# Moving the division of the masked softmax from GpSimd to VectorE in one batch of a fused attention and expert kernel

## The chip, the cores and the metric

The kernel runs on one core of a Trainium2 chip. A core has five engines that work through their own queues of instructions in order: TensorE (PE in the profile, with its weight loads listed apart as PEld), VectorE (DVE), ScalarE (ACT), GpSimd (POOL) and SyncE (SP, which here issues DMAs only). They meet through semaphores. The metric is the device time of one execution in microseconds (us); lower is better.

## The reference

Three layers follow one another. The first is attention with a threshold: a score counts only if it is within `tau` of the row's maximum. Its shape is 2 batches, 8 heads, 576 positions, 64 elements per head.

```python
scores = scale * np.matmul(q, k.transpose(0, 1, 3, 2))
thresh = np.max(scores, axis=-1, keepdims=True) - tau
scores = np.where(scores >= thresh, scores, -1000000000.0)
scores = scores - np.max(scores, axis=-1, keepdims=True)
attn = np.exp(scores)
attn = attn / (np.sum(attn, axis=-1, keepdims=True) + 1e-09)
return np.matmul(attn, v).astype(np.float32)
```

The second layer takes the 1152 tokens of 512 elements through three matrices to 768, keeps the largest of the three results, and multiplies by `w_out` back to 512. The third mixes four experts (512 to 1024, ReLU, back to 512) by normalised probabilities. All of it is float32.

## The kernel before, in words

**Products.** A float32 matrix product is made of three passes over values that are cut into a high and a low part (`split_term`): high by low, low by high, high by high. ACT makes the high part by a copy that rounds, and POOL or DVE makes the low part by a subtraction. For the weights that is `block`: `hi` on ACT (line 780), `lo` on POOL (line 784). For the experts' hidden values it is line 1202 on ACT and line 1205 on DVE; the experts' outputs are added up on DVE (line 1225).

**Stages.** The tokens are worked in two groups. `attention_fast` does batch 0's attention alone. Then comes a stage in which the products of group 0 (the largest-of-three layer, then the experts) run on TensorE, and `attention_slow` weaves batch 1's attention into them. The end is the rest of group 0 and all of group 1. In the middle stage and in the last one the order on TensorE, VectorE, ScalarE and GpSimd is the program's order (`manual_schedule`); only the SyncE queue's order is chosen by the planner.

**Batch 1's attention.** It has four jobs (pairs of heads) of nine tiles each, 36 steps, and one step more to finish. A tile is 128 query rows by 576 keys. A tile goes through `qk` (scores in PSUM, PE, line 416), `peak` (negated row maximum, DVE, 427), `power` (exponential, ACT, 434), `limit` (threshold, DVE, 430), `weigh` (mask by the threshold, with the row's sum as a second result, DVE, 439), `norm` (reciprocal of the sum on DVE, 445, and the multiplication of the tile by it, 446), `turn` (transposes on PE, 456 and 460), `cut_hi` (high parts of the turned tile on ACT, 502 and 504), `cut_lo` (low parts on DVE, 523 and 525) and, when a group of tiles is complete, `gather` (the product with the values, PE, 549, evacuated by 552 on ACT and 554 on DVE).

Each step of `attention_slow` has four quarters, and a `yield` behind each of them hands over to the product stream, which issues 2100 columns of matmuls and, between them, whatever ACT, DVE and POOL instructions of the products and weights are due. In step i tile i goes through `qk` and `peak` (first quarter), `power` and `limit` (second), `weigh` (third) and `norm` (fourth); tile i-1 goes through `turn` (second), `cut_hi` (third) and `cut_lo` (fourth). `advance` issues the next piece of a job's preparation (`prep`, with DVE lines 243, 256, 257, 283) and of what follows a group (`gather`, `values`).

The argument `swift` of `norm` chooses the engine of the multiplication. In batch 1 it is true for the first two tiles only, so these two run on VectorE and 34 on GpSimd. In batch 0 the call is another one, and the change does not touch it.

PSUM has one buffer for the scores of a tile, one for its transposes, two for smaller pieces and the values' products, and three for the product stream.

Of the kernel before, what the change touches and what calls it, by code (L numbers as in the profile page):

```python
# [22 lines left out]
def fused_kernel(ctx: ExitStack, tc: tile.TileContext, q, k, v, tau, w1, w2, w3, w_out, probs, m_w1, m_w2, out):  # L23
# [118 lines left out]
    def whole_tile(key):  # L142
        if key not in whole:
            whole[key] = mo["whole"].tile([P, N1], F32, tag="whole", name="whole", bufs=KC)
        return whole[key]
# [22 lines left out]
    def load_job(job, names="qkv"):  # L168
        b, p = job.b, job.p
        for nm, src in (("q", q), ("k", k), ("v", v)):  # L170
            if nm not in names:
                continue
            heads = src[b, 2 * p:2 * p + 2]
            load = nc.scalar.dma_start if nm == "v" and b else nc.sync.dma_start
            main = heads[:, 0:MAIN, :].rearrange("h (p c) d -> p h c d", c=NC)
            if nm == "v":
                t = atile([P, 2, NC, D], F32, "vnat")
                load(out=t, in_=main)
            else:
                t = atile([P, NC, 2, D], F32, f"{nm}nat")  # L180
                for h in range(2):
                    nc.sync.dma_start(out=t[:, :, h, :], in_=main[:, h])
            if nm == "q":
                r = diagonal
                for h in range(2):
                    last = nc.sync.dma_start(out=r[h * REM:(h + 1) * REM, h * D:(h + 1) * D], in_=heads[h, MAIN:S, :])
            elif nm == "k":
                r = atile([REM, 2, D], F32, "knrem")
                last = nc.sync.dma_start(out=r, in_=heads[:, MAIN:S, :].rearrange("h r d -> r h d"))
            else:  # L190
                r = atile([P, 1 + (b in TWOFOLD), D], F32, "vnrem")
                if b in TWOFOLD:
                    for h in range(2):
                        last = load(out=r[h * REM:(h + 1) * REM], in_=heads[:, MAIN:S, :].rearrange("h r d -> r h d"))
                else:
                    last = load(out=r[:, 0, :], in_=heads[:, MAIN:S, :])
            job.raw[nm] = (t, r)
        return last
# [142 lines left out]
    def values(job, follower=None):  # L341
        V = atile([P, 2, NC, 2 * D], F32R, "V")
        twofold = job.b in TWOFOLD
        if job.b == 0 or job.p == 0 or twofold:
            at["VR"] = atile([P, 2, 2 * D], F32R, "VR")
            if not twofold:
                nc.gpsimd.memset(f32(at["VR"]), 0.0)
        VR = at["VR"]
        job.v = (V, VR)
        vt, vr = job.raw["v"]  # L350
        vn = vt
        nc.scalar.activation(out=V[:, :, :, 0:D], in_=vn, func=AF.Copy)
        yield
        nc.gpsimd.tensor_tensor(out=V[:, :, :, D:2 * D], in0=vn, in1=f32(V[:, :, :, 0:D]), op=ALU.subtract)
        parts = [(slice(0, P), slice(0, 2))] if twofold else [(slice(h * REM, (h + 1) * REM), slice(h, h + 1)) for h in range(2)]
        for r, h in parts:
            nc.scalar.activation(out=VR[r, h, 0:D], in_=vr[r], func=AF.Copy)
        yield
        for r, h in parts:
            nc.gpsimd.tensor_tensor(out=VR[r, h, D:2 * D], in0=vr[r], in1=f32(VR[r, h, 0:D]), op=ALU.subtract)  # L360
        if follower:
            for _ in range(3):
                yield
            load_job(follower, "v")
# [32 lines left out]
    def qk(st):  # L397
        K12, QS = st.grp.job.kq
        nat = st.grp.job.nat
        st.s = ptile_at("S", [P, 2, 512])  # L400
        for kh in range(2):
            terms = []
            if st.h is None and nat:
                KN, QD = nat
                terms = [(QD[:, y, :], KN[:, x, kh * HS:(kh + 1) * HS]) for y in range(2) for x in range(2)]
            elif st.h is None:
                for h in range(2):
                    lhsT = QS[:, (MAIN, W)[h]:(MAIN, W)[h] + 2 * REM]
                    ko = h * (W + REM) + kh * HS
                    terms += [(lhsT, K12[:, x, ko:ko + HS]) for x in range(2)]  # L410
            else:
                qo = (st.c * P, W + 2 * REM + st.c * P)[st.h]
                ko = st.h * W + kh * HS
                terms = [(QS[:, qo:qo + P], K12[:, x, ko:ko + HS]) for x in range(2)]
            for i, (l, r) in enumerate(terms):
                st.whole = nc.tensor.matmul(st.s[:, kh, 0:HS], lhsT=l, rhs=r, start=i == 0, stop=i == len(terms) - 1)  # L416

    def views(st):
        em = st.em[:, st.col:st.col + S]
        return st.s[:, :, 0:HS], em, em.rearrange("p (a b) -> p a b", a=2)  # L420
# [15 lines left out]
    def weigh(st):  # L436

        sv, _, ev = views(st)
        nc.vector.scalar_tensor_tensor(  # L439
            out=ev, in0=sv, scalar=st.stat["thr"], in1=ev, op0=ALU.is_ge, op1=ALU.mult, accum_out=st.stat["sum"])  # L440

    def norm(st, swift=False):
        em = views(st)[1]
        su, re = st.stat["sum"], st.stat["r"]
        nc.vector.reciprocal(out=re, in_=su)  # L445
        last = (nc.vector if swift else nc.gpsimd).tensor_scalar(out=em, in0=em, scalar1=re, scalar2=one, op0=ALU.mult, op1=ALU.mult)  # L446
        if st.h is None and st.grp.job.b not in TWOFOLD:
            nc.gpsimd.tensor_scalar(
                out=st.em[:, S:S + REM], in0=st.em[:, MAIN:S], scalar1=1.0, scalar2=1.0, op0=ALU.mult, op1=ALU.mult)
        return last  # L450
# [138 lines left out]
    def lined_up(jobs):  # L589
        steps = []  # L590
        for j, job in enumerate(jobs):
            new = job_steps(job)
            for r, st in enumerate(new):
                st.job, st.j, st.r = job, j, r
            steps += new
        return steps
# [87 lines left out]
    def attention_slow(jobs, modes):  # L684

        steps = lined_up(jobs)
        n = len(steps)
        front, back = Queue(), Queue()
        for nm in "kqv":
            load_job(jobs[0], nm)  # L690
        yield SETTLE
        front.add(prep(jobs[0]))
        while not jobs[0].ready:
            front.advance()
            back.advance()
            yield PREPARE
        for p in range(NPAIR):
            nc.gpsimd.tensor_scalar(
                out=whole_tile(("x", p))[:, 0:REM], in0=shared[:, p, :], scalar1=1.0, scalar2=1.0, op0=ALU.mult, op1=ALU.mult)
        yield STACKED  # L700
        for i in range(n + 1):
            st = steps[i] if i < n else None
            old = steps[i - 1] if i else None

            def advance():
                front.advance()
                back.advance()

            if i == 1:

                back.add(values(*jobs[0:2]))
            if st:
                while st.job.ready < 1 + (st.h == 1):
                    front.advance()
                if st.j + 1 < len(jobs):
                    if st.r == LOAD_B:
                        load_job(jobs[st.j + 1], "qk")
                    if st.r == PREP_B:
                        front.add(prep(jobs[st.j + 1]))
                qk(st)  # L720
                peak(st)
            advance()
            yield
            if st:
                power(st)
                limit(st)
            if old:
                turn(old)
            advance()
            yield  # L730
            if old:
                cut_hi(old, next(modes) if old.h is not None else "dve")
            if st:
                weigh(st)
            advance()
            yield
            if st:
                norm(st, i < 2)
            if old:
                cut_lo(old)  # L740
                if old.last:
                    back.add(gather(old.grp))
                    if old.r == 2 * NC and old.j + 1 < len(jobs):
                        back.add(values(*jobs[old.j + 1:old.j + 3]))
            advance()
            yield
        while back.q:
            back.advance()
            yield
# [659 lines left out]
```

## Time and profile before

| | |
|---|---|
| median of three runs | 705.01 us (704.23 to 705.45) |
| profiled execution | 705.1 us |
| its span, first to last instruction | 703.3 us |
| PE busy | 688.2 us, 98% |
| DVE busy | 475.5 us, 68% |
| ACT busy | 365.3 us, 52% |
| POOL busy | 487.1 us, 69% |

The profile is one execution as the hardware profiler recorded it. Its page gives each engine's busy time; matmuls are pipelined and their ends are modelled, so the start-to-start distance of two matmuls says more of PE's pace than its busy share. A group of instructions is written as line, engine, operation, output and inputs by the program's names of tiles, shape, and count. A timeline row is the start in us from the span's start, the duration in us, the engine, the line, and what it did. A wait is put down to the instruction that came last by the semaphores' records. The chain of waits follows the end of the execution, or of a stretch, back from each instruction to the one that released it.

### The profile page before, as it was taken

Reading aid. Unit: us, or ns where it says so; the run is one execution under the profiler, and the core shown is the slowest. Engines: PE = TensorE matmul, PEld = TensorE weight load, DVE = VectorE, ACT = ScalarE, POOL = GpSimd, SP = SyncE. Lnnn points to the kernel's source line nnn. Section 1 sums busy time; section 2 is a strip of 40 time slices with the busy share of each in tenths; the row PEclk is TensorE's granted clock in tenths of the full one; section 3 lists DMA queues with packets and bytes.
Section 4 is the critical chain, followed back from the end, with each engine's and each line's share of the span. In section 5 each row is a group of like instructions: output and inputs, shape, how many; then the busy total and the mean of one; then the engine's idle time right before and its main releaser. Section 6 shows DMA issues by size and latency. Waiting matters only on the chain.

```text
span 703.3 us, 11937 instructions
## 1 busy us (share of the span) xinstructions
PE 688.2 (98%) x3975; PEld 613.3 (87%) x3975; DVE 475.5 (68%) x1062; ACT 365.3 (52%) x774; POOL 487.1 (69%) x561
## 2 busy tenths in 40 slices
PE   7999999999999999999999999999999999999997
PEld 6888889887778888888888889999998998998996
DVE  6998898895477767677676567874644644653653
ACT  5989875554455555474655354445533434433430
POOL 4869876765575657576586477778569669669660
PEclk9999999999999999999999999999999999999999
DMA  6764506988878458475443653454222222323103
GB/s 190 172 138 103 152 1 187 280 246 237 220 216 220 120 140 219 121 177 151 122 118 90 213 161 134 137 166 129 59 82 90 88 63 90 91 67 92 52 1 76
DMA packets 108808, 95.17 MB, mean 135 GB/s; under 512 B 27340, under 2 KB 91852, under 8 KB 108748
## 3 DMA queue, kind: packets, MB, share of 16 engines
q1 hardware_dynamic: 91498, 83.24, 42.8%
q10 hardware_dynamic: 17218, 11.18, 5.5%
q8 instruction: 32, 0.52, 0.3%
q14 instruction: 28, 0.23, 0.1%
q0 software_dynamic: 32, 0.00, 0.0%
HBM read 69.09 MB, written 13.37 MB: 117 GB/s over the span
## 4 chain that ended last, share of the span: by engine, by line
PE 72%; DVE 7%; POOL 7%; ACT 6%; issue 4%; DMA 3%; ACTq 0%; SPq 0%; POOLq 0%; DVEq 0%
PE ps L1261 60%; PE u L549 5%; PE s L416 3%; POOL a L784 3%; PE t L456 2%; DMA raw<-in_moe_w_dram 2%; ACT em L434 1%; POOL em L446 1%; DVE raw L824 1%; DVE st_negm L427 1%; DVE em L439 1%; DVE bits L819 1%; DVE hmax L882 1%; DVE bits L813 1%; DMA krem<-in_k_dram 1%
## 5 line engine op out<-in xcount | busy, mean ns | idle before, releaser
L1261 PE MATMUL ps<-b,hh 128*128 128x512 f32 (+1 forms) x584 | 184.3, 389 | 0.0
L784 POOL TENSOR_TENSOR b<-raw,b 128x512 fp32r<-128x512 f32 x64 | 83.0, 1302 | 68.2 <-ACT b L780 68.2
L1261 PEld LDWEIGHTS ps<-b,hh 128*128 128x128 f32 x584 | 108.3, 188 | 20.4
L1261 PE MATMUL ps<-b,hl 128*128 128x512 f32 (+1 forms) x292 | 113.8, 390 | 0.0
L784 POOL TENSOR_TENSOR a<-raw,a 128x512 fp32r<-128x512 f32 (+1 forms) x58 | 72.9, 1259 | 40.7 <-ACT a L780 35.4
L1225 DVE SCALAR_TENSOR_TENSOR acc<-ps,pr,acc 128x512 f32<-128x512 f32 (+1 forms) x64 | 47.4, 741 | 72.7 <-PE ps L1261 72.4
L446 POOL TENSOR_SCALAR em<-em,st_r,one 128x576 f32<-128x576 f32 x68 | 56.4, 830 | 43.7 <-DVE st_r L445 34.6
L434 ACT ACTIVATE em<-s,st_negm 128x576 f32<-128x576 f32 x72 | 53.5, 743 | 59.2 <-DVE st_negm L427 52.1
L1261 PE MATMUL ps<-y0h,a 128*128 128x512 f32 x256 | 83.0, 397 | 0.0
L427 DVE TENSOR_REDUCE st_negm<-s 128x1 f32<-128x576 f32 x72 | 54.2, 754 | 31.5 <-PE s L416 30.7
L1261 PE MATMUL ps<-bt,sh 128*128 128x320 f32 x300 | 70.1, 309 | 0.0
L439 DVE SCALAR_TENSOR_TENSOR em<-s,st_thr,em 128x576 f32<-128x576 f32 x72 | 58.6, 814 | 13.3 <-ACT em L434 12.1
L1046 POOL TENSOR_TENSOR sl<-s,sh 128x512 fp32r<-128x512 f32 x50 | 64.8, 1318 | 0.0
L1261 PEld LDWEIGHTS ps<-b,hl 128*128 128x128 f32 x292 | 54.9, 188 | 10.0
L780 ACT ACTIVATE a<-raw 128x512 fp32r<-128x512 f32 (+1 forms) x66 | 39.5, 603 | 34.7 <-DVE raw L824 11.6
L1033 POOL TENSOR_TENSOR dl<-wraw,dh 128x512 fp32r<-128x512 f32 (+1 forms) x50 | 50.1, 1023 | 8.4 <-ACT dh L1028 8.4
L1152 ACT ACTIVATE hh<-ps 128x320 fp32r<-128x320 f32 x64 | 27.4, 439 | 54.7 <-DVE ps L1079 54.7
L1261 PEld LDWEIGHTS ps<-y0h,a 128*128 128x128 f32 x256 | 47.2, 189 | 8.2
L416 PE MATMUL s<-K,QS 128*128 128x288 f32 x264 | 48.3, 305 | 4.8 <-DMA QS<-knat 1.4
L1261 PEld LDWEIGHTS ps<-bt,sh 128*128 128x128 f32 x300 | 51.2, 188 | 0.0
L1261 PE MATMUL ps<-y0l,a 128*128 128x512 f32 x128 | 51.1, 399 | 0.0
L416 PEld LDWEIGHTS s<-K,QS 128*128 128x128 f32 x264 | 39.8, 189 | 10.0 <-issue 3.9
(228 smaller groups left out, 1728.2 us busy)
## 6 DMA issues: line engine op xcount, KB each, us to landing
raw<-in_moe_w_dram SPq DMA_DIRECT2D x96, 256.0 KB, 2.9
words<-in_moe_w_dram SPq DMA_DIRECT2D x18, 512.0 KB, 4.8
wraw<-in_moe_w_dram SPq DMA_DIRECT2D x16, 512.0 KB, 3.5
kept_w<-raw SPq DMA_DIRECT2D x18, 256.0 KB, 3.2
wraw<-kept_w SPq DMA_DIRECT2D x9, 512.0 KB, 3.9
K<-KN SPq DMA_DIRECT2D x14, 288.0 KB, 5.3
K<-KN SPq DMA_DIRECT2D x14, 256.0 KB, 4.5
sraw<-kept_w ACTq DMA_DIRECT2D x14, 256.0 KB, 3.6
```

The source lines that it names most:

```text
L416: st.whole = nc.tensor.matmul(st.s[:, kh, 0:HS], lhsT=l, rhs=r, start=i == 0, stop=i == len(terms) - 1)
L427: nc.vector.tensor_reduce(out=st.stat["negm"], in_=views(st)[0], op=ALU.max, axis=AX.XY, negate=True)
L434: return nc.scalar.activation(out=ev, in_=sv, func=AF.Exp, bias=st.stat["negm"])
L439: nc.vector.scalar_tensor_tensor(out=ev, in0=sv, scalar=st.stat["thr"], in1=ev, op0=ALU.is_ge, op1=ALU.mult, accum_out=st.stat["sum"])
L446: last = (nc.vector if swift else nc.gpsimd).tensor_scalar(out=em, in0=em, scalar1=re, scalar2=one, op0=ALU.mult, op1=ALU.mult)
L549: at["valued"] = nc.tensor.matmul(pv, lhsT=l, rhs=r, start=i == 0, stop=i == len(terms) - 1)
L780: nc.scalar.activation(out=b["hi"], in_=b["raw"], func=AF.Copy)
L784: nc.gpsimd.tensor_tensor(out=b["lo"], in0=b["raw"], in1=f32(b["hi"]), op=ALU.subtract)
L1033: nc.gpsimd.tensor_tensor(out=rows(b["dl"], x), in0=src, in1=f32(rows(b["dh"], x)), op=ALU.subtract)
L1046: nc.gpsimd.tensor_tensor(out=rows(b["sl"], slice(x, x + 2)), in0=rows(b["s"], slice(x, x + 2)), in1=f32(rows(b["sh"], slice(x, x + 2))), ...
L1225: nc.vector.scalar_tensor_tensor(out=accs[t][:, cols], in0=ps, scalar=pe, in1=accs[t][:, cols], op0=ALU.mult, op1=ALU.add)
L1261: nc.tensor.matmul(banks[x], lhsT=l, rhs=r, start=i == 0, stop=i == count - 1)
```

## The change

`norm` is called in the third quarter, right behind `weigh` and ahead of `advance` and of the `yield`, instead of in the fourth; and it is called with `swift` true for every tile. So in batch 1 the reciprocal and the multiplication stand directly behind the mask in VectorE's queue, and GpSimd has no multiplication of this kind there. Nothing else is edited.

```diff
                 cut_hi(old, next(modes) if old.h is not None else "dve")
             if st:
                 weigh(st)
+                norm(st, True)
             advance()
             yield
-            if st:
-                norm(st, i < 2)
             if old:
                 cut_lo(old)
                 if old.last:
```

The function that it calls is unchanged:

```python
    def norm(st, swift=False):
        em = views(st)[1]
        su, re = st.stat["sum"], st.stat["r"]
        nc.vector.reciprocal(out=re, in_=su)
        last = (nc.vector if swift else nc.gpsimd).tensor_scalar(out=em, in0=em, scalar1=re, scalar2=one, op0=ALU.mult, op1=ALU.mult)
        ...
```

## Rows read from the trace of the kernel before

**Rows 1.** The page: PE's total (busy, share, instructions), its busy slices, its clock

```profile
PE 688.2 (98%) x3975; PEld 613.3 (87%) x3975; DVE 475.5 (68%) x1062; ACT 365.3 (52%) x774; POOL 487.1 (69%) x561
...
PE   7999999999999999999999999999999999999997
...
PEclk9999999999999999999999999999999999999999
```

**Rows 2.** Busy us of each engine (instructions), clock, DMA share, GB/s, 195 to 390 us

```profile
195.00:390.00 195.00, 194.18 (x1057) 165.66 (x1057) 140.35 (x325) 106.42 (x221) 129.47 (x164) 1.00 0.57 154
```

**Rows 3.** Line 446, 195 to 395 us: count, ns min/median/max; below, who waited for it

```profile
L446 POOL TENSOR_SCALAR em<-em,st_r,one x34: 819/828/854, 200.4 to 383.5; 128x576 f32<-128x576 f32 x34
...
  PEld t L456: 2.0, 3
...
  PE t L456: 0.5, 1
```

**Rows 4.** Timeline of PE before two transposes that waited

```profile
208.19 0.39 PE L1261 MATMUL ps<-y0h,a 128*128 128x512 f32 x1
209.10 0.33 PE L456 MATMUL t<-ident,em 128*128 128x128 f32 x1 [0.52 <-POOL em L446]
...
259.32 0.39 PE L1261 MATMUL ps<-b,hh 128*128 128x512 f32 x1
259.80 0.44 PE L456 MATMUL t<-ident,em 128*128 128x128 f32 x2
```

**Rows 5.** Chain of waits, 205 to 215 us: start, us on the chain, what

```profile
207.35 0.69 DVE hl L1205
208.04 0.07 DVE st_r L445
...
213.35 0.77 PE s L416 x4
```

**Rows 6.** Timeline: two multiplications on DVE, and POOL beside the second

```profile
189.54 0.15 DVE L445 RECIPROCAL st_r<-st_sum 128x1 f32<-128x1 f32 x1
189.73 0.58 DVE L446 TENSOR_SCALAR em<-em,st_r,one 128x576 f32<-128x576 f32 x1
...
195.01 1.30 POOL L784 TENSOR_TENSOR a<-raw,a 128x512 fp32r<-128x512 f32 x1
...
195.51 1.12 DVE L446 TENSOR_SCALAR em<-em,st_r,one 128x576 f32<-128x576 f32 x1
```

**Rows 7.** Timeline of DVE and PE, 239.8 to 241.6 us

```profile
239.87 0.16 DVE L445 RECIPROCAL st_r<-st_sum 128x1 f32<-128x1 f32 x1
239.95 0.67 DVE L523 TENSOR_TENSOR am<-t,am 128x512 fp32r<-128x512 f32 x1
240.66 0.61 DVE L525 TENSOR_TENSOR ar<-u,ar 64x128 fp32r<-64x128 f32 x2
...
241.59 0.28 PE L549 MATMUL u<-ar,VR 128*128 128x256 f32 x1
```

**Rows 8.** Timeline of DVE and PE, 268 to 270.2 us

```profile
268.49 0.61 DVE L525 TENSOR_TENSOR ar<-u,ar 64x128 fp32r<-64x128 f32 x2
...
270.19 0.31 PE L549 MATMUL u<-ar,VR 128*128 128x320 f32 x1
```

**Rows 9.** Timeline of POOL, DVE and PE's weight loads, 278 to 285 us

```profile
278.64 1.29 POOL L784 TENSOR_TENSOR b<-raw,b 128x512 fp32r<-128x512 f32 x1 [1.46 <-ACT b L780]
...
279.40 0.16 DVE L445 RECIPROCAL st_r<-st_sum 128x1 f32<-128x1 f32 x1
...
283.06 0.82 DVE L439 SCALAR_TENSOR_TENSOR em<-s,st_thr,em 128x576 f32<-128x576 f32 x1 [0.56 <-ACT em L434]
...
283.80 0.69 DVE L1205 SCALAR_TENSOR_TENSOR hl<-ps,hh 128x512 fp32r<-128x512 f32 x1
...
284.73 0.19 PEld L1261 LDWEIGHTS ps<-b,hl 128*128 128x128 f32 x1
```

**Rows 10.** Waits of ACT, 195 to 395 us: who for whom, us in total, times, longest

```profile
ACT em L434 <- DVE st_negm L427: 46.9, 27, 3.0
```

## The prediction

> **What bounds the kernel now.** I read the page's totals first, then busy time by stretch, the line of the change with who waits for it, the timelines around those waits, and the chain of waits where a saved wait might come back. The totals show PE busy for 98% of the span, with its clock granted in full in every slice of the page [rows 1]. The change touches only the second batch's attention, which runs from about 186 to 393 us, mixed with expert products. In its 195 us from 195 to 390 PE is busy for 194.18 us, DVE for 140.35 us (72%) and POOL for 129.47 us (66%) [rows 2]. So nothing that is saved on POOL, and nothing spent on DVE, counts by itself. What counts is where PE waits for either. Behind that stage PE stays full to its last slice [rows 1], so a microsecond that PE loses or gains here arrives at the end unchanged.
>
> The time is reckoned from the profiled execution, 705.1 us (span 703.3 us), which lies 0.1 us above the median of the three runs, 705.01 us. A run of this kernel can be told from no change at about 0.2%, that is 1.4 us: below 703.6 is faster, above 706.4 slower.
>
> **What the change removes.** 34 divisions leave POOL, 0.83 us each by their median of 828 ns: 28.2 us [rows 3]. PE's transposes waited for them at three places in the stretch: 2.0 us idle on the weight loads and 0.5 us on the matmuls themselves [rows 3]. Part of that idle time is only the loader's usual lead, so I price each place by PE's pitch. Full-width matmuls start about 0.23 us apart. At 209.10 us the first transpose starts 0.91 us behind the matmul before it, which is 0.68 us too late; at 259.80 us it is 0.48 us, 0.25 too late [rows 4]; the third place, at 358.87 us, reads 0.23 the same way. That is 1.16 us together. The division would now end about 0.8 us behind the mask, long before each of these transposes, so all three waits go.
>
> But what is late next? Around the first place the chain of waits doesn't run over PE: it goes from the split of the products at 207.35 us on DVE through the reciprocal there (0.07 us) and on, over DVE and ACT, to the score matmuls at 213.35 us [rows 5]. PE arrives there earlier and waits. Only the reciprocal leaves that chain, so 0.07 of the 0.68 us stays. Gain: 0.07 + 0.25 + 0.23 = 0.55 us; it would be 1.16 us if nothing took it back.
>
> **What the change adds.** DVE carries 34 divisions more. The trace has two that already run there. Undisturbed, one took 0.58 us and began 0.19 us behind the start of its reciprocal; the other took 1.12 us, and it began at 195.51 us while POOL was in a split that ran from 195.01 us for 1.30 us, to 196.31 us. It ended at 196.63 us, 0.32 us behind POOL [rows 6]. So a division costs from 0.58 to about 1.12 us, and I take 0.58 us where no POOL row lies across its start and POOL's end plus 0.32 us where one does. In the old order the next instruction starts 0.08 us behind the reciprocal's start [rows 7], so each tile delays what is queued behind the mask on DVE by 0.58 + 0.19 - 0.08 = 0.69 us, at worst by 1.23 us.
>
> The Trainium skill, page "SBUF — State Buffer", section "SBUF: two separate sides", says that VectorE and GpSimd take a shared pair of ports as an exclusive lock: whichever instruction starts first holds it to its end. That speaks against this change, and the 1.12 us division bears it out. By that rule a division that begins just behind the start of a 1.30 us split would take 1.30 + 0.32 = 1.62 us.
>
> What is queued behind it? In program order the division now stands in front of the products' evacuations, the splits of the turned probabilities (L523, L525) and the next tile's maximum. DVE runs these in order, and 34 x 0.69 = 23.5 us would take it from 72% to 84% of the stretch. Most of the delay falls into idle time. I compared, for every tile, when PE needs what stands behind the division:
>
> - At 240 us the remainder split ends at 240.66 + 0.61 = 241.27 us and PE's value matmul takes it at 241.59 us [rows 7]. Slack 0.32, delay 0.69: PE loses 0.37 us (0.91 at the worst delay).
> - At 269 us the split ends at 269.10 and is taken at 270.19 us [rows 8]. Slack 1.09 us, and the tile before passes its own delay on while DVE has no idle time between: between 0.69 and 1.38 us, a loss of 0 to 0.29. I take 0.15 (1.37 if both tiles pay 1.23).
> - At 284 us lies the dearest place. The last hidden split ends at 283.80 + 0.69 = 284.49 us, and PE loads it as weights at 284.73 us: slack 0.24. Two tiles' delays meet here. The first division would be ready at 279.40 + 0.19 = 279.59 us, but POOL's split runs from 278.64 us to 279.93 us, so it ends at 280.25 us: 0.66 us, a delay of 0.77 [rows 9]. DVE's idle time before the second mask doesn't absorb it, since that mask waits for ACT's exponential [rows 9], and the exponential waits for DVE's maximum [rows 10], which is late by the same 0.77. The second division then stands in front of the hidden split: 0.77 + 0.69 - 0.24 = 1.22 us lost (2.22 at the worst delay).
> - The other tiles have more slack than delay, or fall short by a tenth. I allow 0.3 us for them together, between 0 and 1.
>
> Sum: 0.37 + 0.15 + 1.22 + 0.3 = 2.04 us lost, 0.55 gained, 1.5 us slower: 705.1 + 1.5 = 706.6, and 706.5 beside the median. At the worst delays it is 0.91 + 1.37 + 2.22 + 1 - 0.55 = 4.95 us, about 710. With no new wait and nothing given back it is 705.1 - 1.16 = 703.9.
>
> POOL's 28.2 us I cost at nothing: what POOL does besides is split weights, and no PE row in the stretch waits for those.
>
> **Rivals.** *The waits go and nothing comes.* DVE hides everything, because its queue has 55 us of idle time in the stretch and what I read as passed on dies out earlier. For it speaks that PE shows no wait on DVE above the tightest slacks today; against it the 0.24 and 0.32 us of slack, both smaller than the smallest possible division. 703.9 us with all three waits saved, 704.6 with what the chain leaves of them. Even so it would hardly reach the bound of "faster".
>
> *The lock makes a backlog.* POOL is still busy for (129.47 - 28.2) / 195 = 52% of the stretch, mostly in 1.30 us splits, and with the divisions gone it starts these earlier, into DVE's new ones. If a division takes 1.1 us on the average and not 0.7, DVE passes its delay from tile to tile, and I get the worst sum, about 710 us. It decides from a mean duration of about 1 us. Of the two rows, one was hit.
>
> **Chances.** The forecast's case (one large new wait at about 284 us, some small ones, less than a microsecond won) has 0.57, and its own range is 705.3 to 707.8. Since the bound of "slower" at 706.4 lies inside it, 0.36 of it counts as slower and 0.21 as the same. The first rival has 0.27: 0.21 the same, 0.06 faster, which needs something better than I can price. The backlog has 0.16, all slower. Together: faster 0.06, same 0.42, slower 0.52. The range that should hold the time is 704.4 to 709.0.
>
> **What would show it.** The division on DVE should have a mean of 0.65 to 0.85 us with its shortest at 0.58; POOL should have none from 200 us on and a busy time lower by 28 us. PE's waits for the division at 209, 260 and 359 us should be gone, and the wait at 213 us be there, longer. New should be a PE wait of over 1 us for the hidden split (L1205) at about 285 us and one of 0.3 to 0.6 us for the remainder split (L525) at about 242 us. I am wrong in the largest term if PE has no gap at 285 us, and wrong in kind if PE's busy time in the stretch falls by more than 3 us, or if the time differs with PE as full as before, which would put the cause into another stage or into the order of the loads.

## The result and the profile after

The changed kernel takes 709.32 us in the median of six runs, against 704.47 us for the kernel before beside it. The ratio is 1.0084, with a 95% interval of 1.0069 to 1.0099: slower by about 5.9 us. (The ratio is that of the means of the six, 710.04 and 704.15 us; the medians lie 4.85 us apart.) The profiled execution has a span of 707.5 us, 4.2 us more than the one of before, which at 705.1 us was one of the longer ones of its kernel. The direction was forecast. The size was not: 1.5 us were forecast, and the time lies just above the stated range, which ended at 709.0.

The whole loss lies in the stage that the change touches: the mask of the third tile starts at 198.21 us, 1.07 us earlier than before, the stage's last transposes at 389.11 us, 4.21 us later than before, and the execution ends 4.2 us later. Here is the stretch of [rows 2] after the change (busy us of PE, PEld, DVE, ACT, POOL), and the totals of the page that answer to [rows 1]:

```profile
PE 689.7 (97%) x3975; PEld 613.1 (87%) x3975; DVE 504.7 (71%) x1096; ACT 364.8 (52%) x774; POOL 462.4 (65%) x527
...
195.00:390.00 195.00, 190.38 (x1030) 160.78 (x1029) 165.96 (x351) 103.85 (x214) 102.81 (x128) 1.00 0.57 152
```

In these 195 us PE is busy for 190.38 us instead of 194.18: 3.80 us less. DVE went from 140.35 to 165.96 us, POOL from 129.47 to 102.81. What PE waits for in the stretch (total, times, longest) has changed from the division on POOL [rows 3] mostly to things that stand behind the division on DVE (line numbers shift by a few between the runs: L1204 here, and L1206 or L1207 below, are the hidden split L1205 of before, and L783, L784 and L786 are the same weight split):

```profile
PE t L456 <- DVE am L523: 2.5, 4, 0.8
PE ps L1260 <- DVE hl L1204: 0.8, 1, 0.8
PE u L549 <- DVE ar L525: 0.6, 2, 0.4
PE s L416 <- DVE em L439: 0.5, 1, 0.5
```

The division itself, on line 446, is now on DVE in all 34 tiles of 196 to 395 us. The row gives minimum, median and maximum in ns:

```profile
L446 DVE TENSOR_SCALAR em<-em,st_r,one x34: 578/580/1592, 199.3 to 386.3; 128x576 f32<-128x576 f32 x34
```

The median is the undisturbed 0.58 us, but the mean is 0.84. Seven of the 34 took 1.45 to 1.59 us, each begun 0.01 to 0.16 us behind the start of a split on POOL; they make up three quarters of the excess over 0.58, and divisions of 0.66 to 1.10 us the rest. One of the seven, with ACT and POOL beside it and the PE wait behind it:

```profile
231.97 0.74 ACT L434 ACTIVATE em<-s,st_negm 128x576 f32<-128x576 f32 x1 [3.15 <-DVE st_negm L427]
...
232.61 0.59 ACT L502 ACTIVATE am<-t 128x512 fp32r<-128x512 f32 x1
233.08 0.64 ACT L779 ACTIVATE b<-raw 128x512 fp32r<-128x512 f32 x1
...
233.80 1.28 POOL L783 TENSOR_TENSOR b<-raw,b 128x512 fp32r<-128x512 f32 x1 [2.96 <-ACT b L779]
...
232.74 0.82 DVE L439 SCALAR_TENSOR_TENSOR em<-s,st_thr,em 128x576 f32<-128x576 f32 x1 [0.56 <-ACT em L434]
...
233.81 1.59 DVE L446 TENSOR_SCALAR em<-em,st_r,one 128x576 f32<-128x576 f32 x1
235.32 0.74 DVE L1224 SCALAR_TENSOR_TENSOR acc<-ps,pr,acc 128x512 f32<-128x512 f32 x1
235.98 0.68 DVE L523 TENSOR_TENSOR am<-t,am 128x512 fp32r<-128x512 f32 x1
...
235.42 0.63 PE L1260 MATMUL ps<-y0h,a 128*128 128x512 f32 x2
236.80 0.41 PE L456 MATMUL t<-ident,em 128*128 128x128 f32 x2 [0.76 <-DVE am L523]
```

POOL had been idle for 2.96 us when ACT's copy of a weight block ended (233.08 + 0.64 = 233.72). Its split of that block started at 233.80 us, 0.01 us ahead of DVE's division, and the division ended at 235.40 us, 0.32 us behind the split. The products' evacuation and the split L523 of the turned tile stood behind it on DVE; PE's next transposes need the PSUM buffer that L523 empties, and waited 0.76 us.

The same tile in the kernel before, POOL and DVE:

```profile
234.46 0.82 POOL L446 TENSOR_SCALAR em<-em,st_r,one 128x576 f32<-128x576 f32 x1 [2.04 <-DVE st_r L445]
235.25 1.30 POOL L784 TENSOR_TENSOR b<-raw,b 128x512 fp32r<-128x512 f32 x1
...
233.53 0.75 DVE L1225 SCALAR_TENSOR_TENSOR acc<-ps,pr,acc 128x512 f32<-128x512 f32 x1
234.19 0.15 DVE L445 RECIPROCAL st_r<-st_sum 128x1 f32<-128x1 f32 x1
234.26 0.67 DVE L523 TENSOR_TENSOR am<-t,am 128x512 fp32r<-128x512 f32 x1
```

There POOL waited 2.04 us for the reciprocal, and its split of the same weight block stood behind the division in its queue, until 235.25 us. Taking the division from POOL took this wait away too. POOL now starts the split as soon as ACT has copied the block, and ACT copies it shortly behind the exponential that also releases the mask on DVE, here with one other instruction (L502) between. So mask, reciprocal and division on one side, copy and split on the other, run off from one event. In five of the seven cases POOL was released by a copy that began 1.04 to 1.12 us behind the exponential.

What POOL waits for in the stretch (total, times, longest) shows that this is the rule now. Before, first line, it was mostly the reciprocal, with 25 us in 16 waits for ACT's copies besides; after, the two lines below, it is the copies:

```profile
POOL em L446 <- DVE st_r L445: 29.7, 18, 4.2
...
POOL a L783 <- ACT a L779: 41.0, 17, 6.0
POOL b L783 <- ACT b L779: 37.1, 20, 3.8
```

### The profile page after: what moved, and what is told of

The parts are those of the page before. It is cut to its first block, busy times and chain, and to the rows that moved or that the text cites. A ratio compares the mean times of both kernels' runs of the same rounds, so it can differ in the third digit from the quotient of the medians.

```text
span 707.5 us, 11907 instructions
## 1 busy us (share of the span) xinstructions
PE 689.7 (97%) x3975; PEld 613.1 (87%) x3975; DVE 504.7 (71%) x1096; ACT 364.8 (52%) x774; POOL 462.4 (65%) x527
## 4 chain that ended last, share of the span: by engine, by line
PE 76%; DVE 7%; ACT 5%; POOL 4%; DMA 4%; issue 3%; ACTq 0%; SPq 0%; POOLq 0%; DVEq 0%
PE ps L1260 65%; PE u L549 5%; PE s L416 3%; PE t L456 2%; DMA raw<-in_moe_w_dram 2%; DVE em L439 2%; ACT em L434 2%; DVE st_negm L427 1%; DVE em L446 1%; DVE am L523 1%; DMA krem<-in_k_dram 1%; POOL em L446 1%; POOL a L783 1%; DVE hl L1204 1%; DMA knat<-in_k_dram 1%
## 5 line engine op out<-in xcount | busy, mean ns | idle before, releaser
L783 POOL TENSOR_TENSOR b<-raw,b 128x512 fp32r<-128x512 f32 x64 | 83.2, 1305 | 92.2 <-ACT b L779 90.4
L783 POOL TENSOR_TENSOR a<-raw,a 128x512 fp32r<-128x512 f32 (+1 forms) x58 | 73.3, 1267 | 75.2 <-ACT a L779 71.6
L1038 ACT ACTIVATE sh<-s 128x512 fp32r<-128x512 f32 x50 | 29.9, 625 | 32.9 <-POOL s L977 32.9
```

The lines of the kernel that those rows point to most:

```text
L783: nc.gpsimd.tensor_tensor(out=b["lo"], in0=b["raw"], in1=f32(b["hi"]), op=ALU.subtract)
L1038: nc.scalar.activation(out=rows(b["sh"], slice(x, x + 2)), in_=rows(b["s"], slice(x, x + 2)), func=AF.Copy)
```

## Experiments

Ratios are to the kernel before on the same chip, in five rounds, with the 95% interval behind them. The runs whose names begin with e, with f and g, and with h were taken on three different chips, so they are compared with each other by their ratios only.

**Theories at the start.** Q: what costs is the division's place in DVE's queue, ahead of the splits L523, L525 and L1205. L: DVE's added load costs by its amount, wherever it stands. S: the move itself costs, through the order of loads.

**e_move: moved, but left on GpSimd.**

```diff
                 weigh(st)
-                norm(st, True)
+                norm(st, i < 2)
             advance()
```

> The call of norm is moved behind the mask as in the change, but the division of the 34 tiles stays on GpSimd; only the reciprocal is early on VectorE. Theory Q (what costs the time is the division standing in VectorE's queue ahead of the splits of the turned tile and of the hidden values): VectorE has no more work than before, so nothing is lost; GpSimd's division can start earlier, so PE's waits for it (1.16 us at three places before) shrink: ratio to before 0.998 to 1.000. Rival L (VectorE's added load costs, wherever it stands): 0.998 to 1.000 too, no load is added. Rival S (the move itself, through the order of the loads on SyncE or of the queue, costs): about 1.006 to 1.008 as in the changed kernel.

Measured: 0.9985 (0.9971 to 0.9999), 702.69 against 703.12 us. S falls: the move costs nothing. The early reciprocal even takes PE's waits for the division away. In its profile PE waits in the stretch for one thing only, 0.4 us at a mask, and is busy for 194.60 us. This version beats both kernels, by an amount close to what a measurement can tell.

**e_late: on VectorE, at the old place.**

```diff
             if st:
-                norm(st, i < 2)
+                norm(st, True)
             if old:
                 cut_lo(old)
```

> All 36 divisions on VectorE, but the call stays in the fourth quarter, behind the product stream's work and directly ahead of cut_lo. Q: the hidden split (L1205) is no longer behind the division, so PE's gap of 1.0 us at about 286 us goes; the splits L523 and L525 still are, so PE's waits for them (2.5 and 1.1 us idle in the changed kernel) stay: ratio 1.003 to 1.007. L: 1.006 to 1.010, as the changed kernel. A third theory, that only standing right behind the mask matters: 0.998 to 1.001.

Measured: 1.0087 (1.0065 to 1.0109). PE's gap at the hidden split shrank to 0.2 us (the matmul at 286.83 us comes 0.43 us behind the one before), as Q had it, but the whole loss came out as large as in the changed kernel, above Q's range. The division's mean was 0.87 us, its longest 1.67.

**e_behind: on VectorE, behind the splits.**

```diff
-            if st:
-                norm(st, i < 2)
             if old:
                 cut_lo(old)
+            if st:
+                norm(st, True)
+            if old:
                 if old.last:
```

> All 36 divisions on VectorE, in the fourth quarter but behind cut_lo, so neither the splits of the turned tile nor the hidden split stand behind the division; only the next tile's maximum does. VectorE's load is that of the changed kernel. Q: PE's waits for L523 and L525 go, no PE wait of 0.5 us for VectorE is left but at the score matmuls: ratio 0.998 to 1.002. L: 1.006 to 1.010.

Measured: 1.0112 (1.0091 to 1.0134), the slowest of all. Q is wrong as a whole. The waits for L523 and L525 went, as it said, but others took their place (who waited, total us, times, longest):

```profile
PE t L456 <- DVE em L446: 4.3, 4, 1.8
PE ps L1262 <- DVE hl L1206: 0.4, 1, 0.4
```

PE now waited for the division itself, whose mean was 0.93 us and whose longest 1.70. Wherever the division stands, its long cases come out on PE. L is left, or a theory of the long cases.

**e_none: no division.**

```diff
                 weigh(st)
-                norm(st, True)
+                norm(st, True, i >= 2)
```

(The third argument, added to `norm`, makes it return behind the reciprocal.)

> The 34 divisions are left out altogether (the reciprocals stay, at the new place), so the output isn't normalised there. It prices the gain that was there to be had. Q and L alike: PE's three waits for GpSimd go, what the chain at 213 us takes back stays: 0.5 to 1.2 us faster, ratio 0.9983 to 0.9993. If it is faster by more than 2 us, the divisions cost more before than PE's visible waits.

Measured: 0.9995 (0.9981 to 1.0010), just above the expected range. It agrees with a gain of about a microsecond or less and can't be told from none, nor from e_move. In its profile PE's waits for POOL are gone, but it waits 1.0 us at two other places (202 and 208 us) for the split of the turned tile on DVE. So the division on POOL held no hidden microseconds that came out at the end; what the new waits took back wasn't measured apart.

**K: the long divisions are the cause.** The next four tell L from K, by which a division costs as much as it does because it has to wait for the GpSimd instruction in flight.

**f_after and f_before: short splits on GpSimd.** One edit in both, active from the third tile of batch 1 to its end (the lines that switch `"brief"` on and off are left out here):

```diff
+            cut = slice(0, 16) if "brief" in at else slice(0, shape[-1])
             nc.gpsimd.tensor_tensor(
-                out=b["lo"], in0=b["raw"], in1=f32(b["hi"]), op=ALU.subtract)
+                out=b["lo"][..., cut], in0=b["raw"][..., cut], in1=f32(b["hi"])[..., cut], op=ALU.subtract)
+            if "brief" in at:
+                b["lo"] = b["hi"]
```

> The changed kernel, with GpSimd's weight splits cut to 16 columns of each 128 or 512 from the third tile of batch 1 to its last one (the products take the high part in place of the low one there, so the low parts of these weights are left out). VectorE's work is unchanged. Theory K (the division costs so much because it waits for the GpSimd instruction in flight: 0.58 us alone, up to 1.59 us behind a 1.30 us split, mean 0.85): with short splits the mean is 0.58 to 0.65 us, none over 1.0, and most of the loss goes: ratio to before 0.998 to 1.003. Rival L (34 x 0.58 us of work on VectorE cost by themselves, where PE has no slack against VectorE): ratio 1.005 to 1.008.

> The control: the kernel before with the same cut of GpSimd's weight splits (same part left out). K and L alike: PE's waits for GpSimd's division shrink, nothing else moves: ratio 0.997 to 1.000. The effect of the change without long splits is f_after against this one.

Measured: f_after 1.0016 (1.0004 to 1.0028), f_before 0.9993 (0.9983 to 1.0004). VectorE's instructions are those of the changed kernel, but all 34 divisions are short:

```profile
L446 DVE TENSOR_SCALAR em<-em,st_r,one x34: 578/579/595, 198.3 to 381.6; 128x576 f32<-128x576 f32 x34
```

Between the two the change costs 0.23%, about 1.6 us (their intervals leave some 0.5 to 2.7), instead of 5.9.

**g_load58 and g_load85: the load without the wait.**

```diff
                 weigh(st)
                 norm(st, i < 2)
+                if i >= 2:
+                    nc.vector.tensor_reduce(
+                        out=atile([P, 1], F32, "st_junk"), in_=ident[:, None, 0:102].to_broadcast([P, 4, 102]), op=ALU.max, axis=AX.XY)
```

(g_load85 has 7 times 96 elements.)

> The division of the 34 tiles stays on GpSimd (reciprocal early, as in e_move, which gave 0.9985), and VectorE does a maximum over 408 elements of a constant tile in each of these steps right behind the mask, about 0.55 to 0.6 us by the 0.75 us that 576 elements take at line 427, with nothing that waits for it. That is the division's own work on VectorE without its wait for GpSimd: its duration should be constant. K: ratio 0.999 to 1.003. L: 1.005 to 1.008.

> As g_load58 with 672 elements, about 0.85 us: the mean duration that the division has in the changed kernel, but the same in every tile. If only the mean load on VectorE counts (L): 1.007 to 1.010, as the changed kernel. K (what counts are the long ones of 1.45 to 1.6 us at places with little slack): 1.001 to 1.005.

Measured: g_load58 1.0016 (1.0003 to 1.0029), with an added instruction of 0.558 us; g_load85 1.0034 (1.0021 to 1.0048), with one of 0.833 us. The stretch of g_load85 is the sharpest test of L:

```profile
195.00:390.00 195.00, 193.21 (x1046) 163.84 (x1045) 165.70 (x358) 105.68 (x218) 128.60 (x163) 1.00 0.57 154
```

DVE is as busy as in the changed kernel (165.70 against 165.96 us), in the same place, with nearly the same mean. But the load is even, and PE loses 194.18 - 193.21 = 0.97 us of busy time and not 3.80. L falls as the whole cause. Measured from e_move, which has the gain already, the even load costs 0.49% of the 0.99% that the change costs: about half of the loss is the load at its mean. That the other half is its unevenness is what is left by this run; h_gate tests it.

**h_gate: GpSimd waits for the division.**

```diff
                 norm(st, True)
+                if i >= 2:
+                    nc.gpsimd.tensor_scalar(
+                        out=atile([P, 1], F32, "st_junk"), in0=st.em[:, st.col:st.col + 1], scalar1=1.0, scalar2=1.0, op0=ALU.mult, op1=ALU.mult)
             advance()
```

> The changed kernel, with one tiny GpSimd instruction added behind each of the 34 divisions that reads one column of the divided tile, so that GpSimd's queue stops until VectorE's division is done, as it stopped for the reciprocal before. In the changed kernel six divisions of 1.45 to 1.59 us began 0.02 to 0.16 us behind the start of a 1.30 us weight split: both are released by ScalarE, the mask by the exponential, the split by the weight copy that ScalarE makes next. Theory K: with the gate the split that is next in the queue starts behind the division and not in front of it. The long divisions go but for those that meet a split or sum already in flight; mean below 0.72 us, and the ratio to before falls from 1.0084 to 1.001 to 1.004 (g_load58 1.0016, g_load85 1.0034). If the long divisions were not the cause of the half that g_load85 leaves open, the ratio stays at 1.006 to 1.010.

Measured: 1.0012 (0.9999 to 1.0025). DVE does all that it does in the changed kernel, and POOL's splits have their full length; the moment at which they may start is held back, by 34 added POOL instructions of 0.19 us. Of 34 divisions one is long (1.575 us), one took 1.15 us, and the mean is 0.63. (The expectation counts six long ones in the changed kernel; with the one of 1.448 us, 0.16 us behind a split's start, they are seven.) The tile from above:

```profile
232.92 0.58 DVE L446 TENSOR_SCALAR em<-em,st_r,one 128x576 f32<-128x576 f32 x1
...
233.59 0.19 POOL L737 TENSOR_SCALAR st_junk<-em 128x1 f32<-128x1 f32 x1 [1.81 <-DVE em L446]
233.73 1.29 POOL L786 TENSOR_TENSOR b<-raw,b 128x512 fp32r<-128x512 f32 x1
```

The split now stands behind the division. The largest wait left is the one that the prediction put first:

```profile
283.81 0.68 DVE L1207 SCALAR_TENSOR_TENSOR hl<-ps,hh 128x512 fp32r<-128x512 f32 x1
...
283.16 0.61 PE L1263 MATMUL ps<-b,hh 128*128 128x512 f32 x2
284.55 0.50 PE L1263 MATMUL ps<-b,hl 128*128 128x512 f32 x1 [0.78 <-DVE hl L1207]
```

**h_gate_behind: the gate on e_behind.** The same three lines behind the division there.

> The same gate on e_behind (division on VectorE in the fourth quarter behind cut_lo, which gave 1.0112 with a mean division of 0.92 us and PE waiting 4.3 us for the division itself). K: the mean falls below 0.75 us, and so does the loss: ratio 1.001 to 1.005; PE's waits for the division shrink to under 2 us. If instead the place behind cut_lo is bad by itself, because the transposes need the divided tile that much sooner, the ratio stays above 1.007.

Measured: 1.0049 (1.0031 to 1.0067), from 1.0112; the division's mean fell from 0.93 to 0.63 us. (The expectation's 0.92 counts one division of the second tile besides.) So the long divisions were about half of that version's loss too. But PE still waits 2.8 us for the division, twice, more than expected. The longer wait, 2.0 us at 208.71 us, is for a division of 0.58 us: the place behind the splits is also bad by itself, since one transpose needs the tile that soon. The other, 0.8 us, is for one of 1.47 us.

## Why the prediction was wrong

**What bounds the kernel** held. PE sets the time, and what PE lost in the stage arrived at the end: its last transposes there are 4.2 us late, and so is the end of the span. But the prediction had put down a fall of PE's busy time in the stretch by more than 3 us as the sign of being wrong in kind, and it fell by 3.80.

**The gain.** The three waits of [rows 4] and the third one at 359 us went, and e_move shows what that is worth alone: 0.15%, about 1 us, where I had 0.55 with what the chain of [rows 5] takes back and 1.16 without. The interval allows both. The wait that the chain forecast is there: PE's score matmuls, which didn't wait before, wait 0.5 us at 212 us in the changed kernel.

**The cost of one division is the step that failed.** I took "0.58 us where no POOL row lies across its start and POOL's end plus 0.32 us where one does", read from POOL's rows of before, and so a delay of 0.69 us for nearly every tile. The mechanism was right: each of the seven long divisions ends about 0.32 us behind a split, like the one in [rows 6]. The rows were the wrong ones. In the old trace POOL's splits lie where POOL's own wait for the reciprocal had put them, and the change removes that wait. I costed POOL's freed 28.2 us at nothing. They were not: POOL's idle time before splits now ends with ACT's copy, which comes shortly behind the exponential, as the division does. h_gate gives that wait back to POOL, and the loss falls from 0.84% to 0.12%.

How much the rows of before hide can be estimated from the two traces. In the changed kernel the division starts 1.05 to 1.07 us behind the start of the mask. Put there in the trace of before, tile by tile and by the rule above, the 34 divisions average 0.68 us, and two of them exceed 1.4 us; 0.84 us and seven were measured. So the rows of before already held two long ones (the same two tiles are among the seven), and my worst delay of 1.23 us, taken from the one hit of 1.12 us, left them out: the 1.62 us of a division just behind a split's start was worked out and didn't go into the sum. The other five came with the change itself.

**The sum** was right for divisions of 0.58 us. Where there are only such, f_after against f_before, the change costs about 1.6 us beside the 1.5 predicted. Its terms are borne out in part only: the one wait listed for PE in that stretch of f_after is 0.8 us at the hidden split, and none is listed at 240 or 269 us. In h_gate the wait at the hidden split shows as 0.78 us idle, and the matmul comes 284.55 - 283.16 = 1.39 us behind the start of two that take 0.23 us each, so 0.93 us late; the term was 1.22. In the changed kernel it reads 0.85 us idle, 1.0 us by the starts. The forecast of a PE wait for L525 near 242 us came true as well, with 0.3 us idle.

**The allowance of 0.3 us for the other tiles** is where the failed step came out. There the slack of the transposes' PSUM buffer, which L523 empties, was used up: four waits for L523 and 2.5 us of idle time, three of them behind divisions of 1.45 to 1.59 us and one behind a division of 0.99 us.

**The rival that I gave 0.16**, a backlog by the port lock with POOL's splits starting earlier into DVE's divisions, was the true one in its cause. Its price, about 710 us, came near, but by luck: it stood on a mean of about 1 us, and the mean was 0.84, which by itself costs what g_load85 costs, 0.34%. The rest is the spread: seven divisions two and a half times as long as an undisturbed one, or more.

The Trainium skill, page "SBUF — State Buffer", section "SBUF: two separate sides", has it that GpSimd and a VectorE instruction in a two-port mode, or with two inputs in SBUF, take a shared pair of ports as a lock for a whole instruction, and the one that starts first keeps it. The runs here agree in the main: the division took 0.58 to 0.60 us with short splits on GpSimd, and 1.59 us when a 1.28 us split had started 0.01 us before it. But within a tenth of a microsecond the recorded starts don't tell which of the two is first. Three divisions in e_late and e_behind began 0.02 to 0.07 us ahead of a split and still ended 0.32 us behind it, like this one of e_late:

```profile
264.00 1.63 DVE L446 TENSOR_SCALAR em<-em,st_r,one 128x576 f32<-128x576 f32 x1
...
264.02 1.29 POOL L784 TENSOR_TENSOR a<-raw,a 128x512 fp32r<-128x512 f32 x1 [2.44 <-ACT a L780]
```

## What to carry to other kernels

When an engine is relieved of an instruction, ask what that instruction was holding back: its queue waited there, and what stands behind it can now start earlier, at a moment that some other event sets. A trace of before doesn't show collisions between instructions whose start the change itself moves; look for the event that will release both, and count the steps from it on either side. And an added load on an engine with slack is priced by its longest cases at the tightest places as well as by its mean: the same 166 us of DVE time cost PE 0.97 us of busy time when the added part came evenly and 3.80 us when it came in lumps.

## What was not expected of the hardware

The collisions go both ways. A split on POOL that starts while a division runs on DVE is lengthened: in the changed kernel this one started 0.22 us behind the start of a division of 0.58 us and took 1.52 us, where 1.29 is usual.

```profile
228.90 1.52 POOL L783 TENSOR_TENSOR a<-raw,a 128x512 fp32r<-128x512 f32 x1 [0.93 <-ACT a L779]
```

The extra is small because little of the division was left. This split ended 1.16 us behind the division. Three others, begun 0.28 to 0.40 us behind a division's start, took 1.34 to 1.44 us and ended 1.14 to 1.16 us behind it. So here too the end is set by the end of the other.

A maximum over a constant SBUF tile on DVE, which g_load85 and g_load58 run in the division's place, shows no wait for POOL. Only four of the 34 in g_load85 began while a split of full length ran, one of them 0.27 us into it (a division of e_behind with the same lead took 1.34 us). Most of the others met a division on POOL, which began about 0.2 us behind them. Yet minimum, median and maximum of the 34 lie within 4 ns:

```profile
L737 DVE TENSOR_REDUCE st_junk<-ident x34: 831/833/835, 200.0 to 384.1; 128x1 f32<-128x672 f32 x34
```

So it is not reading SBUF as such that waits. Which property of an instruction does was not tried any further in these runs.
